# Edge blocks, Toeplitz copies, warm-up and instruction order in a convolution with routed experts

## The chip, the cores and the metric

The kernel runs on one core of a Trainium2 chip. The metric is the device time of one execution in microseconds (us), the median of several runs. The core has TensorE (PE; its weight loads are listed as PEld), VectorE (DVE), ScalarE (ACT), GpSimd (POOL) and SyncE (SP), each with a queue of its own that it works through in order, and 16 DMA engines. SP and POOL issue all transfers of this kernel: SP on the hardware queue, POOL on the software queue.

## The reference

```
x: 8 batches x 4160 positions x 192 channels, float32; weight: 8 heads x 7 taps
w = softmax(weight) over the taps                  # 24 channels belong to a head
y[b, s] = sum over k of w[h, k] * x[b, s - 6 + k]  # causal, zeros ahead of position 0
score[b, s] = y[b, s] . w_gate
for each batch: the 128 positions with the highest score
    h = max(y[top] @ w1, 0); ye = h @ w2           # 192 -> 1024 -> 192
    y[top] += sigmoid(score[top]) * ye
```

All of y is the output; only 128 rows of each batch are changed by the expert network.

## The kernel before

**Tiles.** A batch's 4160 positions are one edge block of 128 positions at its start and two groups of 18 windows of 112 positions. A group is written (b, g) here: (0,0), (0,1), (1,0), ... (7,1), 16 in all. A group lies in one of 10 buffers `xb`, a window's 118 positions (6 ahead of it) on the partitions, loaded by one DMA of 1728 KB (`load`). The buffers of the first six groups are used again by the last six. The 8 edge blocks lie together in `eb`.

**Convolution (`add_conv`, `add_edge`).** Per head a 128 x 128 matrix `toep` holds the seven weights along its diagonals. One product per head and group multiplies it with the head's 24 channels of 18 windows (432 columns); three PSUM banks (`pc`) take turns, and ScalarE copies each bank back into `xb`. The first group was cut into 10 and 18 - 10 windows (`CUT`), in two loads, and its first three heads in two products. The edge blocks take 8 products of 192 columns. In the trace a product is two records.

**Matrices.** VectorE and GpSimd make the taps' softmax and a `band` of shifted weights. Four products with selection matrices spread it over the partitions into two banks `pb` (two products each); from each bank, VectorE copies two of four 32-partition strips into `toep` and ScalarE the other two. `WARM` products on zeros run on TensorE ahead of this.

**Scores, search, expert network.** VectorE multiplies each window with `w_gate` and sums (`junk`, 18 per group, 8 for the edge blocks). When all scores of a batch are there, its search (`add_topk`) finds the 128th highest score by counting on ScalarE, TensorE and VectorE in turn, and the row indices `ix`. Then (`add_expert`) POOL gathers the rows from the output in DRAM (`xe`), TensorE transposes and multiplies by `w1s` and `w2s` (`px`, `ph`, `py`), and POOL scatters the result back. A gather reads the output, so it waits until the batch's two stores and the edge store have landed.

**Order.** Every operation is listed in `O` (class `Order`), and `SEQ` gives for each engine the order of the kinds: k constants, v convolution, x edge blocks, s scores, A to H the search of batch 0 to 7, a to h its expert network; on POOL ("G") l is a load; on SP z is a load of w1 or w2, p the edge store, w a group's store. `O.plan` merges the five strings by estimated times (`t0`, `since`, the costs in `add`) into one program; the strings alone fix each engine's order. The start, before the plan, issues `wt`, (0,0), `wg` and `eb` on SP and (0,1) on POOL.

Of the kernel before, what the change touches and what calls it, by code (L numbers as in the profile page):

```python
# [8 lines left out]
F32 = mybir.dt.float32  # L9
# [12 lines left out]

SEQ = {
    "PE": (
        "v10x8v19A2v3Av2AvAv2Av3A2v3Av3B2Av3Bv2BAv2AvBAv2Bv2B2v3BAv2Bv3Bv3BC2vBv2Cv4Cav2Ca3Cav3BC2a3Cav2Cv3D2"
        "a5Dv2CDa3v2Dv3CvbDv3D2Cv2DbCb2Dv3Dbv2DE2vDv2Ev5EvDcvc2Ec4Ecvcv2E2v2F2Eb2c2Fc3Eb3Eb7FEc3vEFv2FdvEvF2"
        "v3Fv4FGdGd3FGd2edGFd3FGd5GdeFe3G2eH2eGe2HGe2He2Ge2He2GfHGf2H2f2GHf2Hf2Hf4Hf2gHf2g3Hg11hg2h16"
    ),
    "A": (
        "v7x8v19A3v3Av2AvAv5A3v3Av3B3v3BAv2ABv2Bv5B3v2Bv3Bv3Bv3C3v4Cv2aC2v3a2v2C4vav3CvD4v3DCv3Dv3bv2D3vDv2D"  # L30
        "v3Dbv2bE3v5Ev2EcEvc2v3cvE3F3E2bFEv2Fv2Fvdv3F3v4Fv3FG3dGFGd2Ge2G3HeHGeHGHGHfH2fH2f2Hg4h4"
    ),
    "V": (
        "k13x3s7x3s29A2xA3s10A4s4A2s4As5A6s13ABABAxB3s8B4AsAs5BA3BAB2s4B2AB3As3A3s2BsBs4A2B2sAs5B2s2C3BC2BsB4"
        "C4sBs7C2s4aCBs2Cs5C5s11BC3B2as6DCD4s7D2sDs6CD2Cs2Das4D2s7bsCD2Cs2D3C6D2sCsCsCD2s2DsEsE3sD2Es5DsDbs2"
        "D2s2E2D2EDs9EsEs3DEs7E2cD2s4FEFcEsE2F2EFs15E3s4F2sEF2s4E2s5Es2bEFEFs3cEFE4F5EsEFs2EG3sFs4dFsGsGs3F2"
        "s7Gs2GsGFsGF2s5GF2Gs3FGdGF2sF2Gs2GFsGF2GdHGH3eH2G2HGH3GH2eH3G3H3G2HeHGH2GHG3H3G2H3GfH3fH10fH3g3h3"
    ),
    "G": (
        "l8al2blalcldlbecfdgehfgh"  # L40
    ),
    "SP": (
        "zpw2zw14"
    ),
}
LAT = {"PE": 197.0, "A": 162.0, "V": 135.0, "G": 150.0, "SP": 0.0, "Q": 0.0}
# [1 line left out]

RATE, BACK = 320.0, 340.0
FRESH = range(10)  # L50
WARM = 11


class Op:
# [123 lines left out]
def tile_conv_moe(ctx: ExitStack, tc: tile.TileContext, x, weight, w_gate, w1, w2, out, cap: int):  # L178
# [156 lines left out]
    HP = H // 4  # L335
# [31 lines left out]
    for j in range(HP):  # L367
        V.tensor_reduce(out=band0[:, j], in_=wp[:, j], axis=AX.X, op=ALU.add)
    V.tensor_tensor(out=band, in0=band0, in1=wr[:, :, None].to_broadcast([P, HP, NCc]), op=ALU.mult)
    HH = H // 2  # L370
    for half in range(2):
        pb = pf.tile([P, 512], F32, tag="pf", name=f"pb_{half}")
        for j in range(2):
            q = 2 * half + j
            PE.matmul(
                pb[:, j * HP * NCc : (j + 1) * HP * NCc], r32[:, q, :], band.rearrange("p j c -> p (j c)"),
                start=True, stop=True,
            )
# [167 lines left out]
    def add_conv(b, g):  # L546
        xt = xb[slot[b, g]]
        evs = []
        pss = [None] * H


        parts = [(h, 0, NI) for h in range(H)]
        if not evacs:
            parts = [(h, *c) for c in ((0, CUT), (CUT, NI)) for h in range(3)] + parts[3:]
        mms = {}
        for h, w0, w1 in parts:
            def mm(h=h, w0=w0, w1=w1):
                if w0 == 0:
                    pss[h] = pc.tile([P, 512], F32, tag="pc", name=f"pc_{b}_{g}_{h}")
                PE.matmul(  # L560
                    pss[h][:M, w0 * GC : w1 * GC].rearrange("p (w c) -> p w c", c=GC),
                    toep[: M + HALO, h, HALO : HALO + M], xt[: M + HALO, w0:w1, h * GC : (h + 1) * GC], start=True, stop=True,
                )

            m = O.add(
                "PE", pe((w1 - w0) * GC), mm, load_ops[b, g], kind="conv", takes="pc" if w0 == 0 else None, b=b,
                since=15000.0 if (b, g) == (0, 1) else 0.0,
            )
            mms.setdefault(h, []).append(m)
        for h in range(H):  # L570
            def ev(h=h):
                A.copy(xt[:M, :, h * GC : (h + 1) * GC], pss[h][:M, : NI * GC].rearrange("p (w c) -> p w c", c=GC))

            e = O.add("A", ca(NI * GC), ev, mms[h], kind="conv", drops="pc", b=b)
            evacs.append(e)
            evs.append(e)
        evac_ops[b, g] = evs
        score_ops[b, g] = [
            add_score(xt, 1 + NI * g + w, w, [evs[-1]], "score", b) for w in range(NI)
        ]  # L580

    def add_edge():

        evs = []
        for h in range(H):
            ps = {}
# [9 lines left out]
            m = O.add("PE", pe(B * GC), mm, [], kind="edge", takes="pc", since=17000.0)  # L596
# [278 lines left out]
    def add_expert(b, t, n, io):  # L875
# [4 lines left out]
        def add(eng, cost, fn, deps, **k):  # L880
            return O.add(eng, cost, fn, deps, kind=kind, b=b, **k)
# [42 lines left out]
        for f0 in range(0, NF, 4):  # L924
            mm = None
            for f in range(f0, f0 + 4):
                def h1(f=f, f0=f0):
                    if f == f0:
                        T["ph", f0] = pf.tile([P, 512], F32, tag="pf", name=f"ph_{b}_{t}_{f0}")
                    o = T["ph", f0].rearrange("p (f s) -> p f s", f=4)[:, f - f0, :n]  # L930
                    fs = slice(f * P, (f + 1) * P)
                    for c in range(DC):
                        PE.matmul(o, w1s[:, c, fs], T["xT"][:, c, :n], start=(c == 0), stop=(c == DC - 1))

                deps = [xo] + ([mm] if mm else [])
                mm = add("PE", 4 * 146.0 * n / P, h1, deps, takes="pf" if f == f0 else None)
# [83 lines left out]
```

## Time and profile before

| | |
|---|---|
| median of 3 runs | 206.16 us (206.03 to 206.88) |
| profiled execution | 204.77 us, its span 203.0 us |
| mean granted TensorE clock | 0.965 of full speed |
| busy: PE, DVE, ACT, POOL | 183.6, 159.4, 137.3, 44.0 us |
| moved by DMA | 58.15 MB, mean 286 GB/s |

The span goes from the first to the last instruction; the rest of the execution's time lies around it. Durations are in us, or in ns where marked. A line number is of little use here, because a helper issues every instruction (L189): the rows are told apart by their tiles, written out<-in. A row of the timeline gives start, length, engine, operation, tiles, form, the count of records merged in it, and in brackets the idle time ahead of it with what ended it. An engine name with a q is its queue of issues.

### The profile page before, as it was taken

The page shows a single profiled execution, that of the slowest core. Times are in us where ns is not written, and L with a number is a line of the kernel's source. Part 1 is how long each engine was busy: PE and PEld are TensorE (multiplying, and loading weights), DVE is VectorE, ACT ScalarE, POOL GpSimd, SP SyncE. Part 2 cuts the span into 40 slices and gives each one's busy share as a digit, 9 for nine tenths or more (in the row PEclk, how much of TensorE's full clock was granted, in tenths as well). Part 3 has the DMA queues.
Part 4 walks back from the last instruction along what each step waited for, and adds up shares of the span by engine and source line. Part 5 has one row for each costly group of instructions (what it writes and reads, how often), then busy time and mean ns, then how long its engine had stood idle before and what let it go on. Part 6 is the DMA issues. An engine that isn't in the chain of part 4 may idle for free. (4 is left out here: it accounts for less than half of the span.)

```text
span 203.0 us, 3660 instructions
## 1 busy us (share of the span) xinstructions
PE 183.6 (90%) x929; PEld 125.2 (62%) x929; DVE 159.4 (79%) x1099; ACT 137.3 (68%) x333; POOL 44.0 (22%) x85
## 2 busy tenths in 40 slices
PE   7396599998999998999999999999999989989990
PEld 2272574453554554575755655877656878879990
DVE  4690039999977997999998999999999997887200
ACT  2035157798999898787897897777789739462220
POOL 8987220000000033000304400320220110111311
PEclk9759679999999999999999999999999999999999
DMA  3999999999999999999999999999899999500100
GB/s 104 300 316 262 313 329 349 387 379 383 386 383 375 342 339 290 360 384 371 314 299 364 355 387 373 330 282 334 305 314 303 273 290 283 174 22 25 38 20 19
DMA packets 45284, 58.15 MB, mean 286 GB/s; under 512 B 1027, under 2 KB 39057, under 8 KB 45264
## 3 DMA queue, kind: packets, MB, share of 16 engines
q1 hardware_dynamic: 38464, 29.82, 47.3%
q0 software_dynamic: 6800, 28.11, 39.8%
q8 instruction: 7, 0.11, 0.2%
q14 instruction: 13, 0.11, 0.2%
HBM read 31.58 MB, written 26.35 MB: 285 GB/s over the span
## 5 line engine op out<-in xcount | busy, mean ns | idle before, releaser
L189 PE MATMUL pc<-xb,toep 118*112 118x432 f32 (+2 forms) x262 | 103.6, 537 | 0.7 <-ACT toep L189 0.5
L189 DVE SCALAR_TENSOR_TENSOR junk<-xb,wg 128x192 f32<-128x192 f32 x288 | 85.6, 352 | 0.3 <-ACT xb L189 0.3
L189 ACT COPY xb<-pc 112x432 f32<-112x432 f32 x128 | 61.7, 517 | 11.7 <-PE pc L189 10.9
L189 PEld LDWEIGHTS pc<-xb,toep 118*112 118x112 f32 x262 | 44.2, 183 | 33.0 <-issue 23.5
L189 ACT ACTIVATE sg<-rep,nb 128x592 bf16<-128x592 f32 (+1 forms) x48 | 36.3, 756 | 12.4 <-DVE j L189 11.7
L189 PE MATMUL ph<-xT,w1s 96*128 96x128 f32 x256 | 35.0, 282 | 0.0
L189 PEld LDWEIGHTS ph<-xT,w1s 96*128 96x128 f32 x256 | 31.1, 191 | 1.1 <-issue 0.5
L189 POOL DMA_INDIRECT xe<-out_dram,ix x8 | 8.2, 1022 | 101.8 <-DVE junk L189 62.6
L189 PE MATMUL py<-w2s,hT 128*128 128x192 f32 x128 | 24.8, 335 | 0.0
L189 DVE DVE_READ_ACCUMULATOR junk<-xb,wg 128x1 f32 x288 | 23.6, 82 | 0.0
L189 PE MATMUL tot<-gm,cnt 128*128 128x18 f32 x64 | 21.2, 337 | 2.6 <-ACT sg L189 2.2
L189 POOL DMA_DIRECT2D xb<-in_x_dram x16 | 19.4, 1219 | 8.6 <-PE pe L189 5.0
L189 PEld LDWEIGHTS tot<-gm,cnt 128*128 128x128 f32 x64 | 12.0, 188 | 14.0 <-ACT sg L189 11.7
L189 PEld LDWEIGHTS py<-w2s,hT 128*128 128x128 f32 x128 | 20.3, 190 | 0.0
L189 POOL DMA_INDIRECT out_dram<-res,ix x8 | 8.0, 997 | 43.9 <-DVE j L189 27.2
L189 DVE SCALAR_TENSOR_TENSOR j<-tot,inc 128x18 f32<-128x18 f32 x64 | 10.8, 174 | 6.6 <-PE tot L189 5.0
L189 ACT ACTIVATE hT<-ph 128x512 f32<-128x512 f32 x16 | 9.5, 593 | 9.4 <-PE ph L189 9.4
L189 ACT COPY rep<-pt 128x296 f32<-128x296 f32 x30 | 10.8, 412 | 5.1 <-PE pt L189 3.0
L189 PEld LDWEIGHTS <-e 128*128 128x128 bf16 x128 | 9.0, 97 | 6.6 <-issue 3.7
L189 PE MATMUL pt<-ex,e 128*128 128x148 bf16 x128 | 11.1, 227 | 1.5 <-DVE ex L189 1.4
L189 ACT ACTIVATE sg<-rep,b 128x592 bf16<-128x592 f32 (+1 forms) x16 | 12.1, 757 | 0.5
L189 DVE SCALAR_TENSOR_TENSOR junk<-eb,wg 128x192 f32<-128x192 f32 x8 | 2.5, 354 | 12.6 <-ACT eb L189 12.6
(110 smaller groups left out, 167.0 us busy)
## 6 DMA issues: line engine op xcount, KB each, us to landing
xb<-in_x_dram POOLq DMA_DIRECT2D x14, 1728.0 KB, 22.3
out_dram<-xb SPq DMA_DIRECT2D x16, 1512.0 KB, 22.1
xb<-in_x_dram POOLq DMA_DIRECT2D x1, 1632.0 KB, 14.3
xb<-in_x_dram SPq DMA_DIRECT2D x1, 960.0 KB, 6.6
xb<-in_x_dram SPq DMA_DIRECT2D x1, 768.0 KB, 8.4
eb<-in_x_dram SPq DMA_DIRECT2D x1, 768.0 KB, 16.8
w1s<-in_moe_w_dram SPq DMA_DIRECT2D x1, 768.0 KB, 21.3
out_dram<-eb SPq DMA_DIRECT2D x1, 768.0 KB, 20.7
```

Source lines behind the costliest of these rows:

```text
L189: return tc.keep_in_program_order(f(*a, **k))
```

## The change

The edge blocks are loaded and stored by one DMA per batch, 8 each way, where one DMA took all. The edge products, evictions and scores stand behind both groups of batch 0 in the order. The first group is one load and one product per head. The loads of w1 and w2 stand behind the stores of (0,0) and (0,1) on SP, and are listed with the edge store as what they come after. The matrices' four products go to four banks (three `pf`, one `pm`), and each bank is copied by one engine. There are 24 warm-up products. The load of (4,1) stands behind batch 0's gather on POOL ("l7al3" for "l8al2"). The strings for PE, A and V are new throughout, with the planner's estimates that they belong to.

```diff
     "PE": (
-        "v10x8v19A2v3Av2AvAv2Av3A2v3Av3B2Av3Bv2BAv2AvBAv2Bv2B2v3BAv2Bv3Bv3BC2vBv2Cv4Cav2Ca3Cav3BC2a3Cav2Cv3D2"
+        "v16x8v8A2v2Av2Av2Av2Av2A2v3Av3Av2Av2AB2v2BAv2Bv2BAv2Bv2B2v3Bv2Bv3Bv3CvCvBvCv2aCBa2Ca3BCv2C2a3vCv2Cva"
...
     "G": (
-        "l8al2blalcldlbecfdgehfgh"
+        "l7al3blalcldlbecfdgehfgh"
     ),
     "SP": (
-        "zpw2zw14"
+        "pwzwzw14"
     ),
...
-WARM = 11
+WARM = 24
...
-    CUT = 10
-    load(0, 0, 0, CUT)
-    load(0, 0, CUT, NI)
+    load(0, 0, 0, NI)
     SP.dma_start(wg, w_gate.partition_broadcast(P))
-    SP.dma_start(eb, bass.AP(x[0].tensor, x[0].offset, [[D, P], [S * D, B], [1, D]]))
+    for b in range(B):
+        SP.dma_start(eb[:, b, :], x[b][:P, :])
...
-    HH = H // 2
-    for half in range(2):
-        pb = pf.tile([P, 512], F32, tag="pf", name=f"pb_{half}")
-        for j in range(2):
-            q = 2 * half + j
-            PE.matmul(
-                pb[:, j * HP * NCc : (j + 1) * HP * NCc], r32[:, q, :], band.rearrange("p j c -> p (j c)"),
-                start=True, stop=True,
-            )
...
-            (A.copy if q > 1 else V.tensor_copy)(
...
+    for q in range(4):
+        pb = (pf if q < 3 else pm).tile([P, 512], F32, tag="pf" if q < 3 else "pm", name=f"pb_{q}")
+        PE.matmul(pb[:, : HP * NCc], r32[:, q, :], band.rearrange("p j c -> p (j c)"), start=True, stop=True)
+        pv = pb[:, : HP * NCc].rearrange("p (h c) -> p h c", c=NCc)
+        for k in range(4):
+            rows, lo, hi = slice(32 * k, 32 * k + 32), 32 * k, min(P, 32 * k + NCc)
+            (A.copy if q % 2 else V.tensor_copy)(toep[rows, HP * q : HP * q + HP, lo:hi], pv[rows, :, : hi - lo])
...
-        parts = [(h, 0, NI) for h in range(H)]
-        if not evacs:
-            parts = [(h, *c) for c in ((0, CUT), (CUT, NI)) for h in range(3)] + parts[3:]
...
-        dst = out[:, :P, :].rearrange("b p d -> p b d")
+        def st():
+            for b in range(B):
+                SP.dma_start(out[b][:P, :], eb[:, b, :])
...
     add_loads()
-    add_weights()
...
         if k == 1:
             add_edge()
+            add_weights()
```

## Rows read from the trace of the kernel before

**Rows 1.** The page: span, busy time by engine, two groups (count, busy, mean).
```profile
span 203.0 us, 3660 instructions
PE 183.6 (90%) x929; PEld 125.2 (62%) x929; DVE 159.4 (79%) x1099; ACT 137.3 (68%) x333; POOL 44.0 (22%) x85
...
L189 PE MATMUL ph<-xT,w1s 96*128 96x128 f32 x256 | 35.0, 282 | 0.0
...
L189 PE MATMUL py<-w2s,hT 128*128 128x192 f32 x128 | 24.8, 335 | 0.0
```

**Rows 2.** Stages: stretch, length, busy of PE, PEld, DVE, ACT, POOL (count); clock, DMA share, GB/s.
```profile
12.00:22.00 10.00, 6.37 (x19) 3.93 (x18) 3.56 (x30) 3.49 (x8) 6.40 (x25) 0.84 1.04 273
22.00:28.00 6.00, 5.47 (x17) 5.49 (x18) 0.00 (x0) 2.23 (x7) 1.23 (x1) 0.50 1.04 327
32.00:62.00 30.00, 28.99 (x105) 14.64 (x103) 28.32 (x201) 26.01 (x60) 0.00 (x0) 1.00 1.05 380
```

**Rows 3.** The chain of waits: the last piece of group (7,1)'s scores.
```profile
165.01 0.28 DVE junk L189 x2
```

**Rows 4.** Timeline of TensorE, 0 to 42 us.
```profile
1.24 4.14 PE L189 MATMUL pw<-xb 128*128 128x512 bf16 x11 [1.24 <-DVE xb L189]
8.77 1.96 PE L189 MATMUL pb<-band,xb 128*128 128x76 f32 x8 [3.39 <-DVE band L189]
11.23 7.14 PE L189 MATMUL pc<-xb,toep 118*112 118x240 f32 x20 [0.50 <-ACT toep L189]
22.53 5.46 PE L189 MATMUL pe<-eb,toep 128*128 128x192 f32 x16 [4.16 <-DMA eb<-in_x_dram]
27.78 14.24 PE L189 MATMUL pc<-xb,toep 118*112 118x432 f32 x38
```

**Rows 5.** Timeline of ScalarE: first matrix copies; first eviction of (1,0).
```profile
10.63 0.55 ACT L189 COPY toep<-pb 32x152 f32<-32x152 f32 x2 [4.37 <-DVE toep L189]
...
35.54 0.52 ACT L189 COPY xb<-pc 112x432 f32<-112x432 f32 x1 [0.21 <-PE pc L189]
```

**Rows 6.** Timeline of VectorE: its first score.
```profile
28.38 0.36 DVE L189 SCALAR_TENSOR_TENSOR junk<-eb,wg 128x192 f32<-128x192 f32 x1 [12.61 <-ACT eb L189]
```

**Rows 7.** DMA issues of 5 to 9 us (KB, us to landing); two in the timeline.
```profile
xb<-in_x_dram POOLq DMA_DIRECT2D x1, 1728.0 KB, 16.6
eb<-in_x_dram SPq DMA_DIRECT2D x1, 768.0 KB, 16.8
...
w1s<-in_moe_w_dram SPq DMA_DIRECT2D x1, 768.0 KB, 21.3
...
5.61 0.44 SPq L189 DMA_DIRECT2D eb<-in_x_dram  x1
...
5.59 1.46 POOL L189 DMA_DIRECT2D xb<-in_x_dram  x1
```

**Rows 8.** Timeline of POOL: batch 0's gather, the loads behind, the last load.
```profile
74.43 1.07 POOL L189 DMA_INDIRECT xe<-out_dram,ix  x1 [44.43 <-DVE junk L189]
75.48 2.51 POOL L189 DMA_DIRECT2D xb<-in_x_dram  x2
...
131.07 1.31 POOL L189 DMA_DIRECT2D xb<-in_x_dram  x1
```

**Rows 9.** Store (0,1): its issue on SP, and its us to landing.
```profile
35.36 23.35 SPq L189 DMA_DIRECT2D out_dram<-xb  x1
...
out_dram<-xb SPq DMA_DIRECT2D x1, 1512.0 KB, 38.0
```

**Rows 10.** Landing of the loads issued at 75.48 and 131.07 us.
```profile
xb<-in_x_dram POOLq DMA_DIRECT2D x1, 1728.0 KB, 15.4
...
xb<-in_x_dram POOLq DMA_DIRECT2D x1, 1632.0 KB, 14.3
```

**Rows 11.** Timeline of TensorE: into (4,1); first products of (7,1).
```profile
80.67 3.13 PE L189 MATMUL pc<-xb,toep 118*112 118x432 f32 x8
...
147.63 0.96 PE L189 MATMUL pc<-xb,toep 118*112 118x432 f32 x2
```

More of the change, by code (lines that the diff above doesn't have):

```diff
@@ L24 @@
     "PE": (
-        "v10x8v19A2v3Av2AvAv2Av3A2v3Av3B2Av3Bv2BAv2AvBAv2Bv2B2v3BAv2Bv3Bv3BC2vBv2Cv4Cav2Ca3Cav3BC2a3Cav2Cv3D2"
-        "a5Dv2CDa3v2Dv3CvbDv3D2Cv2DbCb2Dv3Dbv2DE2vDv2Ev5EvDcvc2Ec4Ecvcv2E2v2F2Eb2c2Fc3Eb3Eb7FEc3vEFv2FdvEvF2"
-        "v3Fv4FGdGd3FGd2edGFd3FGd5GdeFe3G2eH2eGe2HGe2He2Ge2He2GfHGf2H2f2GHf2Hf2Hf4Hf2gHf2g3Hg11hg2h16"
+        "v16x8v8A2v2Av2Av2Av2Av2A2v3Av3Av2Av2AB2v2BAv2Bv2BAv2Bv2B2v3Bv2Bv3Bv3CvCvBvCv2aCBa2Ca3BCv2C2a3vCv2Cva"
+        "CD2va4Dv2DCa3DCv2Dv5DCDv4Dbv2Dbv3Dv2DE2v2Eb3vDEv3DEv4Ev3cvc2vc4E2c2v2F2Eb4Eb4FvEb4FvEc3FdEc5vFv3EF2"
+        "v3Fv5FGdGFd3Gd2FdGdeFd4Ge4GFd4G2eH2Ge3HGe2HeGe2HGeHeGefH2f3HGf2Hf2Hf3Hf3Hfgf2g2Hg12hg2h16"
     ),
     "A": (
-        "v7x8v19A3v3Av2AvAv5A3v3Av3B3v3BAv2ABv2Bv5B3v2Bv3Bv3Bv3C3v4Cv2aC2v3a2v2C4vav3CvD4v3DCv3Dv3bv2D3vDv2D"
-        "v3Dbv2bE3v5Ev2EcEvc2v3cvE3F3E2bFEv2Fv2Fvdv3F3v4Fv3FG3dGFGd2Ge2G3HeHGeHGHGHfH2fH2f2Hg4h4"
+        "v16x8v8A3v2Av2AvAv5A3v4Av2Av2Av2B3v2Bv2BvBv5B3v3Bv2Bv4Bv2C3vCvaC2v2av3C3a2CvCv3D3CDvDv2Dv6Dv2D2v2bD"
+        "v4DvDv2E3vEv3Eb2v4Ev4cvcv3E2c2EF2EFbEvFEFvFvdv5F3v4Fv4FG3FGd3GeGeG3HeHGeHGHGHfH3fH2f2g4h4"
     ),
     "V": (
[L34 to L37, printed above, removed]
+        "k12s5ks26xs5x2A5xs5A4x3s2As4AsAs5A5s4As4xsAs2As8A3s5AB4sBs4A3B3sBs3A2BA3B3As2A2B5s9Bs2B2s4Bs6BC4BCs2"
+        "Bs9B2C3s9C2aBCB2C2B2sBC2BC3Bs10C2s5CDC2D3CDs4D3s3CD2aCsCaD3Cs7DCD4C3s2C2s7bD2s4DCs6Ds3D2E5D3s6E3s6ED"
+        "EDED3sD2E2Ds16Ebs5EF2E2FEF2s4cs2cs4E2s3Es3Es2F2s4FE2Fs6FEFEbEs5EF2E4FcF2sF2s2E2sEs4GFs4GFGFs8G2FdsF"
+        "s4Fs3FG3sGs2F2s3GFGF2dsGsF2s2GsGFGFGFGHdGH4eH2G3H3GHGH2eH2G2H3G2H4eHG3HGH2GHGH2G2H3fH5fH5fH3g3h3"
     ),
     "G": (
-        "l8al2blalcldlbecfdgehfgh"
+        "l7al3blalcldlbecfdgehfgh"
     ),
     "SP": (
-        "zpw2zw14"
+        "pwzwzw14"
     ),
@@ L549, in add_conv, with mm @@
         pss = [None] * H
-        parts = [(h, 0, NI) for h in range(H)]
-        if not evacs:
-            parts = [(h, *c) for c in ((0, CUT), (CUT, NI)) for h in range(3)] + parts[3:]
[L555 to L559, printed above, removed]
+        mms = []
+        for h in range(H):
+            def mm(h=h):
+                pss[h] = pc.tile([P, 512], F32, tag="pc", name=f"pc_{b}_{g}_{h}")
                 PE.matmul(
-                    pss[h][:M, w0 * GC : w1 * GC].rearrange("p (w c) -> p w c", c=GC),
-                    toep[: M + HALO, h, HALO : HALO + M], xt[: M + HALO, w0:w1, h * GC : (h + 1) * GC], start=True, stop=True,
-                )
-            m = O.add(
-                "PE", pe((w1 - w0) * GC), mm, load_ops[b, g], kind="conv", takes="pc" if w0 == 0 else None, b=b,
-                since=15000.0 if (b, g) == (0, 1) else 0.0,
+                    pss[h][:M, : NI * GC].rearrange("p (w c) -> p w c", c=GC), toep[: M + HALO, h, HALO : HALO + M],
+                    xt[: M + HALO, :, h * GC : (h + 1) * GC], start=True, stop=True,
+                )
+            mms.append(
+                O.add(
+                    "PE", pe(NI * GC), mm, load_ops[b, g], kind="conv", takes="pc", b=b,
+                    since=15500.0 if (b, g) == (0, 1) else 0.0,
+                )
             )
-            mms.setdefault(h, []).append(m)
         for h in range(H):
@@ L572, in ev @@
                 A.copy(xt[:M, :, h * GC : (h + 1) * GC], pss[h][:M, : NI * GC].rearrange("p (w c) -> p w c", c=GC))
-            e = O.add("A", ca(NI * GC), ev, mms[h], kind="conv", drops="pc", b=b)
+            e = O.add("A", ca(NI * GC), ev, [mms[h]], kind="conv", drops="pc", b=b)
             evacs.append(e)
@@ L594, in mm @@
                 )
-            m = O.add("PE", pe(B * GC), mm, [], kind="edge", takes="pc", since=17000.0)
+            m = O.add("PE", pe(B * GC), mm, [], kind="edge", takes="pc", since=20500.0)
             def ev(ps=ps, hs=hs):
@@ L603, in add_edge @@
             edge_scores.append(add_score(eb, 0, b, [evs[-1]], "edge", b))
-        dst = out[:, :P, :].rearrange("b p d -> p b d")
+        def st():
+            for b in range(B):
+                SP.dma_start(out[b][:P, :], eb[:, b, :])
         edge_stores.append(
-            O.add("SP", 0, lambda: SP.dma_start(dst, eb), [evs[-1]], kind="back", lat=1590.0, dma=B * P * D * 4 / BACK, cls=3)
+            O.add("SP", 0, st, [evs[-1]], kind="back", lat=1590.0, dma=B * P * D * 4 / BACK, cls=3, nd=B)
         )
@@ L935, in add_expert @@
                 deps = [xo] + ([mm] if mm else [])
-                mm = add("PE", 4 * 146.0 * n / P, h1, deps, takes="pf" if f == f0 else None)
+                mm = add("PE", 4 * 113.0 * n / P, h1, deps, takes="pf" if f == f0 else None)
             def rl(f0=f0):
@@ L991, in tile_conv_moe @@
             add_expert(b, t, n, hold[b][t])
-    t0 = {"PE": 11900.0, "A": 12300.0, "V": 11300.0, "SP": 4500.0, "G": 11500.0, "Q": 0.0, "D": 13500.0, "HW": 4500.0}
+    t0 = {"PE": 10300.0, "A": 11500.0, "V": 11600.0, "SP": 9000.0, "G": 8300.0, "Q": 0.0, "D": 15500.0, "HW": 9000.0}
     for op in O.plan(t0):
```

9 lines of the change are left out of this document (1 added, 8 removed).

## The prediction

> **What bounds the kernel now.** I read the page first, then the stages, the chain of waits, the timelines of the engines in the first 36 us, and the transfers one by one.
>
> The page says that TensorE is busy for 90% of the span and VectorE for 79% [rows 1]. The stage table says where: from 32 to 62 us TensorE has 28.99 of 30 us and VectorE 28.32, while the DMA engines stand at a share of 1.05 [rows 2]. So three resources are full at once, and a gain at the front reaches the end only if all three let it through. The chain of waits is VectorE's scores up to 165.3 (row at 165.01, 0.28 long) [rows 3]; behind them only the last batch's search and expert network follow. So I ask when the last group, (7,1), can start, because its scores are those.
>
> *The front.* TensorE makes 11 warm-up products (1.24 to 5.38), waits 3.39 for the band, makes the matrices' products, and runs (0,0) from 11.23 to 18.37. Then it is idle for 4.16 until the edge blocks have landed, runs their 8 products from 22.53 in 5.46 us, and is not idle again for long [rows 4]. VectorE idles 12.61 until 28.38 [rows 6]; ScalarE's first eviction of (1,0) is at 35.54 [rows 5]. The granted clock is 0.84 over 12 to 22 and 0.50 (that is 1.2 GHz) over 22 to 28 [rows 2]: it fell behind the idle stretch. Edge blocks and load (0,1) land together, 5.61 + 16.8 = 22.4 and 5.59 + 16.6 = 22.2; w1 is behind them in SP's queue and takes 21.3 [rows 7]. From 12 to 22, with these three at once, the DMA moves 273 GB/s; with one load at a time 327 (22 to 28); with loads and stores 380 [rows 2].
>
> *The back.* POOL's queue is in order, and gathers stand in it between loads. The gather of batch 0 at 74.43 is put down to VectorE, idle 44.43 [rows 8]; but store (0,1), issued at 35.36, lands 38.0 later, at 73.4 [rows 9], and that gather needs it. Two more, batches 1 and 3, start 0.8 us behind their second store in the same way. The last load is issued right behind batch 3's gather, at 131.07, and lands 14.3 later, 145.4 [rows 8, 10]; (7,1)'s first product is at 147.63 [rows 11]. So the last load hangs on bytes moved, not on TensorE, and only 2.2 us lie between it and its use.
>
> **The change part by part.**
>
> *Warm-up, 11 to 24 products.* 13 more at 4.14/11 = 0.38 each at most is 4.9 us: they end at 10.3 at the latest, against 8.77 when the band is ready [rows 4], so 1.5 us late; at the full clock from about where it rose before, they cost half and end in front of 8.77. The cover is the wait for load (0,1) below. I take 0 (0 to 1.5 lost).
>
> *Four banks.* Before, ScalarE's first copy waited 4.37, to the end behind VectorE's copies of the same bank [rows 5]. Its two copies of 0.55 us in all per bank (VectorE's are alike) become eight copies of half the columns on each engine, side by side. The first two heads' matrices are there up to 1 us sooner than 11.23; no copy makes TensorE wait, since a head's product takes 0.72. (0,0) as one load and in one piece per head saves three products' starts. All of it ends in front of load (0,1), so 0 as well (up to 1 us gained if that load came by 16).
>
> *Edge blocks and weights.* The edge load is 8 issues of 0.44 [rows 7] instead of one, so its last part leaves SP near 8.7 or later, with nothing queued behind it now; w1 and w2 go behind stores (0,0) and (0,1). Load (0,1) then shares the DMA with the edge blocks alone. From 12 to 22.2 some 2.78 MB moved at 273 GB/s; without w1's part (0 to 0.79 MB, I take 0.6, as it is three quarters through its 21.3 us) 2.18 MB remain: 8.0 us at 273, 6.7 at 327. So (0,1) lands at 18.7 to 20, at worst at 22.2. I take 18.8, the one-load rate, as 768-byte edge packets are few by then.
>
> *Order at the front.* (0,1) runs from 18.8: 8 products, 0.73 apart as in the stretch from 27.78 (19 in 14.24) [rows 4], to 24.6; then 8 edge products, 192 columns against 432, 0.36 each at full clock: 27.5; the first eviction of (1,0) follows one product later, at 28.3, where it was 35.54. That is 7.2 earlier at full clock, 5.0 if the edge products run at half (0.64 each, as before), 0.8 if load (0,1) is not sooner and the clock is as it was. Between (0,0)'s end (10.4 + 5.8 = 16.2) and 18.8 TensorE idles 2.6, less than the 3.39 and 4.16 behind which the clock fell. I take 6.0. VectorE can score (0,0) while TensorE runs (0,1), so its 12.61 shrink by as much.
>
> The Trainium skill, "TensorE: Matmul & The Clock Gate", section "HAM oscillation — how this bites in real kernels", warns that a wait for a transfer between two runs of products drops the array back to its cold clock and makes the next run start slow. The trace agrees for the wait of 4.16 [rows 2, 4]; by that rule (0,1) and the edges would again start at 1.2 GHz, the front would give some 2.6 instead of 6.0, and the sum below would lose 0.4.
>
> *The edge stores, the ninth load, the later order.* Eight edge stores hold SP 3.1 us longer; store (0,0) stands behind them. Before, a store's issue alone stood 23.35 us in SP because the queue was full [rows 9], so 0. Load (4,1) moves from before batch 0's gather to behind it; that gather's stores get one load less ahead of them (1.77 MB, 5.4 us at 327 GB/s), so I expect store (0,1) near 73.4 - 5.4 - 1.5 = 66.5. From there on POOL's and SP's order is as before, as is what TensorE has done by the end of (7,1).
>
> *The DMA's share.* Up to the last load the same bytes must move, so it comes sooner only by what was lost: 10 us at 273 instead of 327 GB/s are 0.54 MB, 1.5 us at the rates of [rows 2]. Bounds: 0 (two read queues stay at 273) to 2.8 (10 us at 380). To this comes the distance between landing and use, 147.63 - 145.4 = 2.2; the edge blocks were used 0.1 behind their landing [rows 4, 7], so up to 2.1 could go. I take 1.5, as the load's small last piece is issued behind its large one.
>
> *The sum.* The end moves by the smaller of front (6.0) and back (1.5 + 1.5): 3.0. The profiled execution took 204.77 us (span 203.0): 201.8. The median shown is 206.16, 1.4 above it; 3.0 less is **203.2**.
>
> **The rivals.**
>
> A. The front is carried whole: 6.0, time 200.2. For it: TensorE has hardly a hole after 27.78, and FFN 0 is issued earlier, so its scatter and the load behind it too. Against: the DMA share of 1.05 and the last load's 2 us. Chance 0.16.
>
> B. The transfers give nothing: the edge packets mix no better than w1's did, the last load lands where it did and is used as late, 206.0 (0 to 0.5 gained). For: w1's 0.79 MB only move elsewhere. Against: 273 GB/s stand alone among the stages. Chance 0.15.
>
> C. Slower: load (4,1) comes too late. If store (0,1) still lands at 73.4, the gather starts at 74.43 and three loads follow at 75.48 instead of two [rows 8]; the first of them lands 15.4 later [rows 10], at 90.9, and (4,1)'s products, at 82.9 before (the seventh of the eight records from 80.67) [rows 11], wait for it. A front 6.0 earlier would wait 14.0. The new order puts 8 more steps of expert network 0 (17 steps take (35.0 + 24.8)/8 = 7.5 [rows 1], so 3.5) and 9 of searches (some 2.2) ahead: 8.3 remain, 2.3 more than the front gave, 208.5. It decides from a store (0,1) landing at 71.1 on. Against: the 5.4 above. Chance 0.14.
>
> The Trainium skill, "DMA: Bandwidth & Descriptors", section "Bandwidth", asks for transfers of 1 MiB or more and gives each a fixed cost of about 2 us in "Anatomy of one DMA". Edge blocks in eight pieces of 96 KB go against it: 8 x 2.2 = 17.8 us one after another, an estimate from that page, instead of 3.8; stores behind would move towards C. No row here has such pieces back to back.
>
> **How the numbers follow.** Forecast 0.55, its own range 201.7 to 204.8 (from 1.4 gained, the distance alone, to 1.5 short of A); A 0.16, B 0.15, C 0.14. One measurement of this kernel tells about 0.5%, 1.0 us, from no change. Forecast and A are faster: 0.71; B is the same: 0.15; C slower: 0.14. The range takes in all of the forecast and B and the near parts of A and C: 200.3 to 206.9.
>
> **What would show it.** Right: load (0,1) landing near 19, TensorE idle there under 3 us with a granted clock of 1.0 behind it; first eviction of (1,0) near 28 to 30; batch 0's gather near 67; last load landing near 144 and used within 0.5 us; the scores' end near 162. Wrong: (1,0) not before 33 (the front failed); a hole on TensorE of several us before (4,1) (C); the last load at 145 or later (B) or before 141 (A).

## The result and the profile after

| | before | after |
|---|---|---|
| median of all runs side by side | 207.45 us (20 runs) | 204.90 us (20 runs) |
| ratio of after to before | | 0.985 (0.981 to 0.989) |
| profiled execution, its span | 204.77, 203.0 us | 201.73, 199.9 us |
| mean granted TensorE clock | 0.965 | 0.985 |

The kernel is 1.5% faster. The forecast was 203.2 of 206.16 us, a ratio of 0.986. The spans differ by 3.1 us, where the sum had 3.0. The same total does not mean the same terms, though, and the two traces differ from the sum in every large one.

Executions of one kernel fall into a faster and a slower group, so each ratio compares the faster ones alone, and the profile of after is that of a second run of the changed kernel (e0 below), because the first fell in the slower group. Medians here are of all runs and spread by a few us; below I compare marks within single traces more than medians.

The stages of after (columns as in [rows 2]):

```profile
12.00:22.00 10.00, 7.94 (x20) 3.57 (x19) 8.83 (x65) 4.88 (x10) 7.30 (x36) 0.89 1.06 327
22.00:28.00 6.00, 4.57 (x12) 2.08 (x11) 1.60 (x13) 2.89 (x6) 0.00 (x0) 0.89 1.05 327
32.00:62.00 30.00, 29.53 (x109) 14.11 (x107) 26.16 (x188) 26.90 (x64) 0.00 (x0) 1.00 1.05 362
```

The DMA moves 327 GB/s from 12 to 22 where it moved 273, VectorE has 8.83 us of work there instead of 3.56, and the clock over 22 to 28 is 0.89 instead of 0.50 [rows 2]. TensorE of after, first the front and then into (7,1):

```profile
1.23 7.80 PE L189 MATMUL pw<-xb 128*128 128x512 bf16 x24 [1.23 <-DVE xb L189]
8.87 1.01 PE L189 MATMUL pb<-band,xb 128*128 128x76 f32 x8
10.39 6.03 PE L189 MATMUL pc<-xb,toep 118*112 118x432 f32 x16 [0.51 <-DMA xb<-in_x_dram]
18.48 7.72 PE L189 MATMUL pc<-xb,toep 118*112 118x432 f32 x16 [2.06 <-DMA xb<-in_x_dram]
27.63 2.89 PE L189 MATMUL pe<-eb,toep 128*128 128x192 f32 x16 [1.43 <-ACT xb L189]
30.36 5.97 PE L189 MATMUL pc<-xb,toep 118*112 118x432 f32 x16
...
144.98 0.69 PE L189 MATMUL pt<-ex,e 128*128 128x148 bf16 x8
145.52 2.37 PE L189 MATMUL pc<-xb,toep 118*112 118x432 f32 x6
```

(0,1) starts at 18.48, idle 2.06 ahead of it. But between the end of (0,1) and the edge products there is a second hole, which the sum did not have. It is put down to ScalarE; ScalarE had been done by then, and the edge blocks' pieces were late. SP's timeline and the list of issues:

```profile
5.77 6.06 SPq L189 DMA_DIRECT2D eb<-in_x_dram  x8
...
eb<-in_x_dram SPq DMA_DIRECT2D x8, 96.0 KB, 9.3
```

The 8 issues take 6.06 us, the last of them near 11.5. Of the first six pieces, four have a landing in the records, 9.3 us behind the issue by the median, and the later the longer (5.9 to 14.7). The last piece's landing is missing in this trace; in the five kernels below whose records hold it (e5, e7, e9, e10, e11) it is at 26.8 to 27.8, and the edge products start 0.3 us behind it each time. ScalarE of after, with the matrix copies (now at once with VectorE's; it waited 4.37 for them in [rows 5]), the edge evictions and the first eviction of (1,0):

```profile
9.47 1.78 ACT L189 COPY toep<-pb 32x76 f32<-32x76 f32 x8 [3.64 <-PE pb L189]
...
28.23 2.65 ACT L189 COPY eb<-pe 128x192 f32<-128x192 f32 x8 [1.48 <-PE pe L189]
31.29 0.52 ACT L189 COPY xb<-pc 112x432 f32<-112x432 f32 x1 [0.41 <-PE pc L189]
```

VectorE of after, its first score (28.38 in [rows 6]) and the end of the last score of (7,1) ([rows 3]):

```profile
17.00 0.36 DVE L189 SCALAR_TENSOR_TENSOR junk<-xb,wg 128x192 f32<-128x192 f32 x1 [0.90 <-ACT xb L189]
...
161.25 0.08 DVE L189 DVE_READ_ACCUMULATOR junk<-xb,wg 128x1 f32 x1
```

POOL of after: the gather of batch 0 with three loads behind it, the last loads, and the tail (gathers `xe`, scatters `res`):

```profile
69.61 1.07 POOL L189 DMA_INDIRECT xe<-out_dram,ix  x1 [49.39 <-DVE junk L189]
70.66 3.72 POOL L189 DMA_DIRECT2D xb<-in_x_dram  x3
...
129.78 1.90 POOL L189 DMA_DIRECT2D xb<-in_x_dram  x2
...
171.49 0.99 POOL L189 DMA_INDIRECT out_dram<-res,ix  x1 [8.01 <-DVE j L189]
178.41 0.97 POOL L189 DMA_INDIRECT xe<-out_dram,ix  x1 [5.93 <-DVE fjunk L189]
181.33 0.99 POOL L189 DMA_INDIRECT out_dram<-res,ix  x1 [1.94 <-DMA xe<-out_dram,ix]
184.55 0.97 POOL L189 DMA_INDIRECT xe<-out_dram,ix  x1 [2.23 <-DVE fjunk L189]
```

From these rows the path can be laid down mark by mark:

| mark | before | after | gained up to here |
|---|---|---|---|
| first eviction of (1,0) | 35.54 | 31.29 | 4.25 |
| first product of (7,1) | 147.63 | 145.52 | 2.11 |
| end of (7,1)'s scores | 165.29 | 161.33 | 3.96 |
| end of the span | 203.0 | 199.9 | 3.1 |

So 4.25 us are gained at the front, not 6.0. Between (1,0) and (7,1) the new order takes 2 us longer, and from (7,1) to the last score 1.85 us less (15.81 for 17.66, of which VectorE is busy 15.53 and 16.96); the last batch's search and expert network then lose 0.9 again. The questions for the experiments: did the front or the last load decide when (7,1) starts, what made the front's size, which edits were worth nothing, and where the 0.9 went.

### The profile page after: what moved, and what is told of

Same layout as the page of the kernel before. It is cut to its first block, busy times and chain, and to the rows that moved or that the text cites. A ratio compares the mean times of both kernels' runs of the same rounds, so it can differ in the third digit from the quotient of the medians.

```text
span 204.0 us, 3714 instructions
## 1 busy us (share of the span) xinstructions
PE 188.1 (92%) x936; PEld 123.9 (61%) x936; DVE 161.2 (79%) x1103; ACT 137.6 (67%) x337; POOL 44.3 (22%) x85
## 3 DMA queue, kind: packets, MB, share of 16 engines
HBM read 31.58 MB, written 26.35 MB: 284 GB/s over the span
## 4 chain that ended last, share of the span: by engine, by line
PE 36%; DVE 8%; DMA 4%; ACT 3%; issue 3%; POOLq 1%; ACTq 0%; DVEq 0%
PE pc L189 18%; PE ph L189 8%; PE py L189 5%; DVE junk L189 3%; PE tot L189 3%; ACT sg L189 3%; DMA out_dram<-res,ix 2%; PE pt L189 2%; DMA xe<-out_dram,ix 1%; DVE j L189 1%; DVE inc L189 1%; POOLq L1005 1%; DVE sv L189 1%; PE pi L189 1%; PE px L189 0%
## 5 line engine op out<-in xcount | busy, mean ns | idle before, releaser
L189 PE MATMUL pc<-xb,toep 118*112 118x432 f32 x256 | 103.2, 538 | 3.9 <-DMA xb<-in_x_dram 2.0
L189 PEld LDWEIGHTS pc<-xb,toep 118*112 118x112 f32 x256 | 41.6, 178 | 35.7 <-issue 25.3
L189 PE MATMUL ph<-xT,w1s 96*128 96x128 f32 x256 | 33.8, 281 | 0.4 <-ACT xT L189 0.4
L189 POOL DMA_INDIRECT xe<-out_dram,ix x8 | 8.4, 1051 | 114.0 <-DVE inc L189 57.2
L189 PEld LDWEIGHTS ph<-xT,w1s 96*128 96x128 f32 x256 | 30.5, 191 | 1.5 <-ACT xT L189 0.9
L189 PE MATMUL py<-w2s,hT 128*128 128x192 f32 x128 | 26.4, 344 | 0.0
L189 PEld LDWEIGHTS py<-w2s,hT 128*128 128x128 f32 x128 | 20.9, 194 | 1.0 <-issue 0.9
L189 PE MATMUL tot<-gm,cnt 128*128 128x18 f32 x64 | 19.9, 315 | 1.5 <-ACT sg L189 1.0
L189 DVE SCALAR_TENSOR_TENSOR j<-tot,inc 128x18 f32<-128x18 f32 x64 | 11.2, 174 | 7.3 <-PE tot L189 5.6
L189 PE MATMUL pt<-ex,e 128*128 128x148 bf16 x128 | 11.9, 231 | 0.3
L189 DVE TENSOR_SCALAR inc<-nb,dj 128x1 f32<-128x1 f32 x48 | 9.8, 209 | 0.6
## 6 DMA issues: line engine op xcount, KB each, us to landing
out_dram<-xb SPq DMA_DIRECT2D x16, 1512.0 KB, 21.4
eb<-in_x_dram SPq DMA_DIRECT2D x8, 96.0 KB, 11.3
```

Source lines behind the costliest of these rows:

```text
L189: return tc.keep_in_program_order(f(*a, **k))
```

## The experiments

Theory F: the front decides, and whatever it gives arrives at (7,1) until the last load lands too late. Theory B (the prediction's rival and its bound): the bytes decide, by the last load's landing. The expectations call this R (rival); from the kernels with fewer bytes on they call B that both limits hold, the later one. The new strings, the four banks and the eight edge stores were not undone by themselves in any run. Diffs are against the changed kernel unless told otherwise.

**The changed kernel again** (e0), for its spread.

> The changed kernel as it is, for a second profile: the first showed the edge products from 28.3 us, 3.6 us of idle TensorE ahead of them, and the clock at 1.2 GHz from 27.3 to 34.1. Theory F (the front decides: the end moves by as much as the first product of (1,0) moves): where the clock stays up there, the edge products take about 2.7 us instead of 5.5, (1,0) starts near 31 instead of 33.5, and the time is about 203. Rival R (the back decides: the last load's landing caps the gain, as the prediction said): the same time with and without the clock's fall, and the last load used within 0.5 us of its landing. Ratio to before 0.981 to 0.989 by both.

Measured: 205.33 us against 208.42, ratio 0.984 (0.974 to 0.994); its profile stands above.

**Edge blocks in one load** (e1).

```diff
-    for b in range(B):
-        SP.dma_start(eb[:, b, :], x[b][:P, :])
+    SP.dma_start(eb, bass.AP(x[0].tensor, x[0].offset, [[D, P], [S * D, B], [1, D]]))
```

> Undoes one part: the edge blocks come in one DMA, as before, the rest stays. F: all its descriptors are queued by 8 us, most edge packets move ahead of load (0,1), the edge blocks are there by 20 us, no wait behind (0,1), (1,0) starts at 27 to 28 us, and the time falls by 3 to 5 us against the changed kernel, to 198 to 200. R: the front gains the same 5 us, but the last load lands within 1 us of where it did and the time falls by less than 1 us. A third: one DMA is no sooner than eight, edge blocks still land near 27, no difference.

Measured: ratio 0.984 (0.979 to 0.990), no different from eight pieces. Its list of issues and its TensorE:

```profile
eb<-in_x_dram SPq DMA_DIRECT2D x1, 768.0 KB, 15.6
```

```profile
19.21 8.99 PE L189 MATMUL pc<-xb,toep 118*112 118x432 f32 x16 [2.84 <-DMA xb<-in_x_dram]
28.03 3.02 PE L189 MATMUL pe<-eb,toep 128*128 128x192 f32 x16
```

Issued at 5.8, the one load lands at 21.4, some 6 us ahead of the last of eight pieces, and the edge products follow (0,1) without a hole. But (0,1) takes 8.99 us instead of 6.0, because most of it ran at half clock, and what the earlier landing gave is gone: (1,0) came at 31.82, so the early front that F and R differ over was not there.

**Eleven warm-up products** (e2).

```diff
-WARM = 24
+WARM = 11
```

> Undoes one part: 11 warm-up products instead of 24. F: (0,0) runs partly at 1.2 GHz and ends near 18, when load (0,1) lands at 18.5, so at most 0.5 us of the front is lost and the edge wait covers it: within 0.7 us of the changed kernel, unless the clock is then low in (0,1) as well, which would cost up to 3 us. R: no difference.

Measured: ratio 0.986 (0.974 to 0.999); part of (0,0) at half clock, and yet the first eviction of (1,0) at 31.69, within 0.4 of after. The 13 products are worth nothing here: with eleven, the last eviction of (0,0) is at 19.45, behind the landing of load (0,1) at 18.2, but the wait for the edge blocks, 2.82 us ahead of their products at 28.04, covers that.

**Load (4,1) back ahead of batch 0's gather** (e3).

```diff
-        "l7al3blalcldlbecfdgehfgh"
+        "l8al2blalcldlbecfdgehfgh"
```

> Undoes one part: load (4,1) again stands ahead of batch 0's gather on POOL (l8al2). F: TensorE's order is unchanged, batch 0's gather comes some 5 us later (near 74 instead of 69.6) as one more load is ahead of its stores, and FFN 0, which the new order has before (4,1), starts up to 3 us later: time up by 0 to 2 us. R: the same bytes ahead of the last load: within 0.5 us.

Measured: 207.46 us (6 runs, too few for a ratio). POOL of this kernel:

```profile
74.25 1.23 POOL L189 DMA_INDIRECT xe<-out_dram,ix  x1 [48.26 <-DVE inc L189]
75.47 2.51 POOL L189 DMA_DIRECT2D xb<-in_x_dram  x2
```

The gather is at 74.25 again, as before the change [rows 8]; with the load behind it, it is at 69.61. The load's 1.77 MB held up store (0,1), as the prediction's 5.4 us said in kind: it landed at 73.3 here and at 68.6 in the first profile of after, whose (1,0) came later still (34.7, and 33.3 here). What it does to the time is not settled.

**The front without holes: one edge load, and products on zeros in the two waits** (e4).

```diff
+    def filler(n):
+        if n:
+            t = pm.tile([P, 512], F32, tag="pm", name="fill")
+            for k in range(n):
+                PE.matmul(t, warm[:, :P], warm, start=True, stop=True)
...
+                if (b, g, h) == (0, 1, 0):
+                    filler(9)
...
+                if h == 0:
+                    filler(2)
```

> The changed kernel with the edge blocks in one DMA, and 9 products on zeros ahead of (0,1)'s first product and 2 ahead of the edges' so that TensorE's clock has no reason to fall in the wait for load (0,1). With the clock up, (0,1) runs from 19 to 25, the edge blocks have landed at 21.4 (as in the run with one load), (1,0)'s first eviction is near 28.5 instead of 31.3. F (the end follows the front): (7,1)'s first product comes 114 us behind that eviction as in the five profiles so far (113.9 to 114.4), near 142.7, and the end is 2.5 to 3 us sooner than in the repeated changed kernel (span 199.9): 197. R (the last load caps it): (7,1) not before 145, no gain.

Measured: 203.76 against 207.83 us, ratio 0.990 (0.983 to 0.997), no different from after. Its front has the 6 us that the prediction asked for, and TensorE now waits for loads, the last time ahead of (7,1) (TensorE, then the last load's line in the list of issues, issued at 129.75):

```profile
16.42 2.11 PE L189 MATMUL fill<-xb 128*128 128x512 bf16 x8
18.96 6.03 PE L189 MATMUL pc<-xb,toep 118*112 118x432 f32 x16 [0.43 <-DMA xb<-in_x_dram]
...
25.26 2.82 PE L189 MATMUL pe<-eb,toep 128*128 128x192 f32 x16
27.91 5.96 PE L189 MATMUL pc<-xb,toep 118*112 118x432 f32 x16
...
84.16 0.95 PE L189 MATMUL pc<-xb,toep 118*112 118x432 f32 x2 [0.86 <-ACT hT L189]
...
109.43 0.95 PE L189 MATMUL pc<-xb,toep 118*112 118x432 f32 x2 [0.28 <-DMA xb<-in_x_dram]
...
145.16 2.40 PE L189 MATMUL pc<-xb,toep 118*112 118x432 f32 x6 [0.50 <-DMA xb<-in_x_dram]
```

```profile
xb<-in_x_dram POOLq DMA_DIRECT2D x1, 1632.0 KB, 14.9
```

The clock was 1.00 over the front and on to (7,1), and the first eviction of (1,0) was at 28.84, 6.7 us earlier than before. After's distance from there to (7,1), 114.2, would have given 143.1; the last loads landed at 144.7 and 145.0, and (7,1) started at 145.16. Of 2.45 us more at the front 0.36 arrived. The last load did not take all of the rest, though: by the first evictions of each group, the lead over after shrinks by 0.9 at (4,1) (the row at 84.16; its load, issued at 69.15 behind batch 0's gather, landed at 84.02, and ScalarE's `hT` ended then too), by some 0.5 at (6,0) (109.43, load landed at 109.3), and the rest goes at the last load, for which TensorE waits 0.50. So the bytes bind at three places here; in after, (4,1) had some 0.5 us to spare.

**The same with fewer bytes (e8), and after with fewer bytes (e9).** In both, the load of (5,0) brings only 9 of its 18 windows, 0.86 MB less, so that part of the output is not the reference's.

```diff
-            ... lambda: load(b, g, 0, NI, G), ...
+            ... lambda: load(b, g, 0, 9 if (b, g) == (5, 0) else NI, G), ...
```

> The kernel with one edge load and filler products, and 0.86 MB less to move: load (5,0) brings 9 of its 18 windows, the others keep an older group's values (so that part of the output is not the reference's). Two limits at once (new theory B: (7,1) starts at the later of the first eviction of (1,0) + 114.2 and the last load's landing + 0.1): the landing moves from 145.0 to about 142.7, the front gives 28.8 + 114.2 = 143.0, so (7,1) starts near 143.1 instead of 145.2, the scores end 15.9 later, near 159, and the time falls by 2 us or a little more. F alone (TensorE only): (7,1) was then already as early as it can be, no change. R alone (bytes only): the same 2.3 us as B.

> The same 0.86 MB less in the changed kernel itself, without the filler and with the edge blocks in eight pieces. B and F: the first eviction of (1,0) stays at 31.3 or later, so (7,1) stays at 145.5 or later (114 behind it); the time falls by at most the end's share, where the last stores drain 2.4 us sooner (0 to 1 us). R alone: (7,1) near 143, time 2.3 us down.

Measured: 202.93 us (no ratio) and 203.07 us (ratio 0.979, 0.973 to 0.984) against 207.93. TensorE and the last load's line (issued at 127.07) with the early front and fewer bytes, and then TensorE with after's front and fewer bytes:

```profile
143.20 0.69 PE L189 MATMUL pt<-ex,e 128*128 128x148 bf16 x8
143.74 2.37 PE L189 MATMUL pc<-xb,toep 118*112 118x432 f32 x6
```

```profile
xb<-in_x_dram POOLq DMA_DIRECT2D x1, 1632.0 KB, 13.6
```

```profile
144.63 0.69 PE L189 MATMUL pt<-ex,e 128*128 128x148 bf16 x8
145.16 2.37 PE L189 MATMUL pc<-xb,toep 118*112 118x432 f32 x6
```

With the early front, the landing of loads was what held (7,1): here the last one lands at 140.7 (144.7 above), the wait for (6,0) is gone too, and (7,1) starts at 143.74, 1.42 us earlier, behind TensorE's own products and with no wait. With after's front the same bytes change next to nothing (145.16 for 145.52, and (1,0) was 0.24 earlier). The two fronts differ by 1.36 us ((1,0) at 29.69 and 31.05) and the two starts of (7,1) by 1.42. So both theories hold, each on its side: (7,1) starts at the later of (1,0) + 114.1 and what the loads allow, of which the last one's landing is the latest. The first of the two limits has more behind it than these two traces: in seven of the traces of the changed order (both of after, e1, e2, e3, e8 and e9) the distance is 114.0 to 114.4 us, with (1,0) anywhere from 29.69 to 34.74; in the others TensorE waits for transfers on the way (e4, and e5, e7, e10 and e11 below). After stands just on the front's side, with the two limits about 0.4 us apart, if its last load, issued at 129.78, landed as the one issued at 129.75 above did (its own landing is not in the records).

The medians of these two kernels do not tell them apart; the rows do. And 0.86 MB less did not move the landing by the 2.3 us expected: against e4's 144.7 it came 4.0 us sooner with the early front, but only 0.4 sooner (144.3) with after's, where the load was issued at 130.36, behind batch 3's gather. So the landing hangs on when that gather lets the load go, and not on the bytes alone.

**More bytes** (e5). The store of (1,0) is issued a second time, into the place of (7,0), 1.55 MB.

```diff
+        def put():
+            SP.dma_start(dst, src[:M])
+            if (b, g) == (1, 0):
+                SP.dma_start(far, src[:M])
```

> The changed kernel with one more store: group (1,0) is stored a second time, to a place of the output that a later store overwrites (1.55 MB, 4.1 to 4.7 us of the DMA engines at 330 to 380 GB/s), behind its own store on SP. F: nothing on TensorE's path is later by more than slack, time within 1 us. R: every load and store behind it is 4 to 5 us later; the last load and (7,1) with them: time 3 to 5 us up. If it is 1 to 3, both limits are close together.

Measured: ratio 1.022 (1.009 to 1.035). POOL and TensorE:

```profile
99.20 1.27 POOL L189 DMA_INDIRECT xe<-out_dram,ix  x1 [24.80 <-DVE d L189]
```

```profile
110.01 0.66 PE L189 MATMUL px<-ident,xe 128*96 128x128 f32 x2 [5.55 <-DMA xe<-out_dram,ix]
```

The gather of batch 1 came at 99.20 (94.56 in after), and TensorE, whose queue is in order, stood 5.55 us at that batch's transposes; the clock fell behind it. (7,1) started at 152.2, 6.7 us late. Bytes ahead of a gather cost more than their own 4.3 us (at the 362 GB/s of after's third stage), so more than either theory had, and by another way: the wait for a gather.

**The kernel before with the weights late** (e6), the one edit alone (against before).

```diff
-        "zpw2zw14"
+        "pwzwzw14"
```

> The kernel before with one part of the change alone: w1 and w2 behind the edge store and stores (0,0), (0,1). Load (0,1) lands near 18.5 to 19 instead of 22.2. The edge blocks, still ahead in TensorE's order and in one DMA, land at 17 to 21. F: the edge products start 2 to 4 us sooner than 22.5, (1,0)'s first eviction moves by as much, and so does the end: ratio 0.98 to 0.99. R: the DMA gain of 1.5 us plus the distance to the last load's use, ratio 0.985 to 0.995.

Measured: 207.04 (4 runs, too few for a ratio) against 207.83 us. TensorE, and the last load's line (issued at 131.93):

```profile
21.40 2.89 PE L189 MATMUL pe<-eb,toep 128*128 128x192 f32 x16 [1.83 <-DMA eb<-in_x_dram]
...
81.23 0.42 PE L189 MATMUL px<-ident,xe 128*96 128x128 f32 x2 [2.14 <-DMA xe<-out_dram,ix]
...
146.69 0.96 PE L189 MATMUL pc<-xb,toep 118*112 118x432 f32 x2
```

```profile
xb<-in_x_dram POOLq DMA_DIRECT2D x1, 1632.0 KB, 13.5
```

This edit alone gives 4.0 us at the front (the first eviction of (1,0) at 31.58) and 0.9 at (7,1). The last load lands where it landed before, at 145.5, but TensorE does not wait for it; what it waits for, in this execution, is batch 0's gather, 2.14 us at 81.23, and the clock is down behind that (0.57 from 83 to 86). From (7,1)'s first product to the last score it takes 17.66 us, exactly as before. So the late weights alone give nearly as much at the front as the whole change (4.25), and the new order's 1.85 us come from the strings. What the edit is worth in time is not settled.

**The changed kernel with the weights early** (e7).

```diff
-        "pwzwzw14"
+        "zpw2zw14"
```

> The changed kernel with that part undone: w1 again right behind the edge loads, the edge store and the rest of SP's order as before the change. Load (0,1) lands at 21 to 22 instead of 18.4, the edge blocks later than 28. F: (1,0)'s first eviction at 34 to 36 and time up by 3 to 4 us against the repeated changed kernel, about the kernel before. R: 1.5 us up.

Measured: ratio 0.997 (0.988 to 1.007). So no gain over the kernel before is shown any more, though the range just reaches that of after (0.981 to 0.989). TensorE in the profiled execution, 209.88 us, the longest of eleven:

```profile
82.58 0.63 PE L189 MATMUL px<-ident,xe 128*96 128x128 f32 x2 [2.60 <-DMA xe<-out_dram,ix]
```

The price did not come where I had looked for it. (0,1) still landed at 17.4; w1 is issued only at 11.2, behind the eight edge issues. Batch 0's gather, issued at 71.29, took 11.1 us (6.2 in after), TensorE waited 2.60 for it, and the clock was at its lower level for 10 us from there. But this is not shown to come from the early weights: the last kernel below, whose program is that of the changed kernel up to this point, has the same in its trace, a gather of 11.3 us and TensorE's wait for it:

```profile
79.85 0.59 PE L189 MATMUL px<-ident,xe 128*96 128x128 f32 x2 [2.00 <-DMA xe<-out_dram,ix]
```

So what the early weights cost, and where, stays open.

**Eight pieces and products on zeros in both waits** (e10; 8 and 13 products).

> The changed kernel with the edge blocks in eight pieces, and filler products alone: 8 ahead of (0,1)'s first product, 13 ahead of the edges'. The clock stays at 2.4 GHz over the front in every run; the edge products still wait for the last pieces, near 27.7, and (1,0)'s first eviction stays at 31.0 to 31.3. B: (7,1) near 145.4, time as in the undisturbed runs of the changed kernel (202 to 203), never with the front of 34.7 that its first profile had.

Measured: ratio 0.985 (0.973 to 0.998), the time of after. The clock stayed at 1.00 over the front, but (1,0) came at 31.72: the edge products waited for the last piece all the same (28.06). Two later waits for transfers, in TensorE's rows,

```profile
106.17 0.42 PE L189 MATMUL px<-ident,xe 128*96 128x128 f32 x2 [0.88 <-DMA xe<-out_dram,ix]
...
121.23 2.40 PE L189 MATMUL pc<-xb,toep 118*112 118x432 f32 x6 [0.29 <-DMA xb<-in_x_dram]
```

make up most of the way from 31.72 + 114.1 = 145.8 to 147.35, where (7,1) started in this one execution; 145.4 had been expected.

**More at the end** (e11). Half of the store of (7,0) goes out twice.

```diff
+        def put():
+            SP.dma_start(dst, src[:M])
+            if (b, g) == (7, 0):
+                SP.dma_start(dst[:, :9], src[:M, :9])
```

> The changed kernel, with half of the store of (7,0) (9 of 18 windows, 0.77 MB) issued a second time right behind it, so that only the last stores grow. Theory: the 0.9 us that the changed kernel loses behind the scores' end (38.6 us from the scores' end to the span's end, against 37.7 before) are lost because batch 6's gather stands in POOL's queue behind batch 3's scatter, whose rows share the DMA with the last stores. Then the scatter lands some 2 us later, batch 6's gather starts 2 us later than its 1.4 us behind the row indices, and the distance from the scores' end to the span's end grows from 38.6 to about 40.6. Rival: the loss lies in the new order of searches on VectorE; then that distance stays at 38.6 whatever the stores do.

Measured: 208.35 us (4 runs, too few for a ratio). In the profiled execution, 209.44 us, the last score ends at 167.12 and the span at 207.35, a distance of 40.2. POOL's tail:

```profile
177.17 0.99 POOL L189 DMA_INDIRECT out_dram<-res,ix  x1 [7.86 <-DVE j L189]
183.84 1.08 POOL L189 DMA_INDIRECT xe<-out_dram,ix  x1 [5.68 <-DVE sv L189]
```

The distance is 1.6 more than in after, near the theory's 2.0, but that decides nothing: without any more bytes at the end it is 38.7 in e9, 39.4 in e4 and 40.8 in e1. Nor did the theory's path come: the scatter of batch 3 and the gather behind it are 6.67 apart (6.92 in after). And row indices of batch 6 are ready 15.6 us behind the last score in both, against 14.9 before (180.20), which no store explains. The distance is 37.7 in both traces of the old order (the kernel before, and the one with the weights late) and at least 38.6 in every trace of the new one, so that part of the 0.9 goes with the new order. Of after's 0.9, 0.5 stands ahead of the last gather (184.55, for 188.04 before) and 0.4 behind it; what makes it stays open.

## Why the prediction was right, and where its terms were not

*Warm-up 0, four banks 0:* right. Copies run side by side, (0,0) starts at 10.39, and load (0,1) covers all of it; eleven products give the same front, there by the cover of the edge blocks' wait. The four banks were not undone by themselves.

*Load (0,1) at 18.8, idle 2.6:* right (landed at 18.3, used at 18.48, idle 2.06), and so is the reason, 327 GB/s with the weights gone: that edit alone took the landing from 22.2 to 18.5 in the kernel before. In the changed kernel the eight edge issues keep w1 away as well (17.4 with the weights early).

*The edge blocks:* this step failed. The prediction had them in SBUF when (0,1) ended at 24.6, "as 768-byte edge packets are few by then". They were half of all packets. In 13 to 18 us of after, the queues moved:

```profile
q0 software_dynamic: 323, 1.41, 88.6%
q1 hardware_dynamic: 321, 0.22, 17.7%
```

Columns are packets, MB and share. The two queues get packet for packet the same number, so the edge pieces of 768 bytes a packet get about a seventh of the bytes beside a load (0.22 of 1.63 MB). The Trainium skill, "DMA: Bandwidth & Descriptors", section "Queues, rings and completion order", says that an engine takes turns between queues by the packet; the trace agrees, 321 to 323 (which records make up one packet in the Trainium skill's sense it does not show). The last piece so landed at 26.8 to 27.8, and the edge products of after were at 27.63 instead of 24.6. One load, whose packets are all queued from the start, landed at 21.4 (e1): from 10 to 12 us, with load (0,1) only starting, its queue moved 0.52 MB, where the eight pieces' queue moved 0.10. The prediction's other reading, eight pieces one after another at some 2 us each, is not what the trace shows: in e9 the first two pieces land 0.3 us apart (11.8 and 12.1), and only the last six, beside the load, 2.1 to 2.4 apart.

*The clock:* the prediction took full speed, since 2.6 us of idle were less than what the clock had fallen behind. This step failed as well; the traces show both cases. In after it was low from 19.9 to 23.3, behind 2.06 us of idle, and the edges ran at full speed; in the first profile of the same kernel it stayed up in (0,1) and fell for the edges, so that (1,0) came at 34.7 and only 0.8 of the front was left. That this is the lowest of the prediction's three values is chance, since that value was for a load (0,1) that is not sooner. TensorE and a stage (clock 0.56) of that first profile:

```profile
18.64 6.03 PE L189 MATMUL pc<-xb,toep 118*112 118x432 f32 x16 [2.04 <-DMA xb<-in_x_dram]
28.28 5.46 PE L189 MATMUL pe<-eb,toep 128*128 128x192 f32 x16 [3.61 <-issue]
```

```profile
28.00:35.00 7.00, 6.72 (x20) 6.03 (x21) 1.84 (x15) 2.81 (x9) 0.00 (x0) 0.56 1.04 327
```

The Trainium skill, "TensorE: Matmul & The Clock Gate", section "HAM oscillation — how this bites in real kernels", the rule that was weighed, would have had both (0,1) and the edges start cold: the edges did in the first profile, (0,1) started at full clock in both and fell 1.4 us into its run in after, and with products on zeros in the waits neither started cold. Length of the wait alone did not decide: of two kernels with the front of after, the edges ran at full clock behind 3.73 us of idle in one (e5, (1,0) at 30.90) and partly at half clock behind 3.78 in the other (e3, 33.30). The front's size is then 7.2 at full clock, less 3.0 for the late edge blocks: 4.2, where I had taken 6.0. The clock cost after nothing, since (0,1) ran its slow part while the edge blocks were still on their way; in the first profile, where it fell later, (1,0) came 3.5 later.

*Eight edge stores 0, load (4,1) behind the gather:* no run undoes the edge stores by themselves, so their 0 is not tested; nor does the row show why a store's issue stood 23.35 us in SP before. The load's move was right in direction: the gather of batch 0 was at 69.6 (forecast 67; 74.43 before), so store (0,1) had landed before the 71.1 from which rival C decides, and C's hole did not come; with the earlier front of e4, (4,1) did wait for that load, by 0.9.

*The back, 3.0:* its two terms were mis-sized against each other. The load's large piece landed at 145.41 before, the small one behind it, which (7,1) needs too, at 145.75, so the distance to the use was 1.9 and not 2.2. Where the load decided (e4), the pieces landed 0.7 sooner, at 144.7 and 145.03, and the distance fell to 0.1 (145.16): 0.7 where 1.5 was taken for the bytes' share, and 1.75 where 1.5 was taken for the distance. Together 2.5, for 3.0.

*The sum, the smaller of front and back:* the rule is right, as the two kernels with fewer bytes show, but at (7,1) the smaller of the two was the front, with 2.1, and not the back, with 2.5. Two terms stood at nothing that were not nothing. First the new order: by "as is what TensorE has done by the end of (7,1)" it was to change nothing, but the way from (1,0) to (7,1) became 2.1 us longer. TensorE is idle there as little as before (2.3 us for 2.5) and has eight more records of the search (`pt`) in it, worth some 0.5; what makes the rest is not shown. In return VectorE has 1.4 us less to do beside the scores from (7,1) on, and these ended 3.96 earlier. The second is the 0.9 lost in the tail. 2.1 + 1.85 - 0.9 = 3.1 is what happened; 3.0 was reached by a smaller back, no new order and no tail. The total was closer than its parts deserved, and that is luck.

*The signs:* load (0,1) near 19, idle under 3 and the scores' end near 162 (161.3) came as said. (1,0) at 28 to 30 was missed by 1.3, the gather near 67 by 2.6, and the clock of 1.0 behind the idle stretch did not hold (0.50 from 20 to 23). "The last load at 145 or later" was named as the sign of B; where the records hold its landing with all bytes moved (e4, e10), it stood near that edge or behind it (144.7, 146.1) without B coming true, since the distance to its use had gone.

## What to carry to other kernels

Where an early start and a late transfer both bound the last stage, lay the two down as times of one mark, and see by how much the second stands behind the first: gains above that are not paid out (here 0.36 of 2.45 us), and look at the loads in between as well as at the last. A transfer in small packets beside one in large ones got its share by packets here, not by bytes, so queue it whole and early, or put nothing large beside it. A gather that lands late stops TensorE in its queue and can take the clock down with it, so look for such waits in each trace before a difference is put down to an edit: the same wait stood in kernels with and without the early weights. When an order is written anew, compare distances between marks along the whole run; work that moves past the mark one looks at changes its time without any gain.

## What the hardware showed that I had not expected

- Two queues with packets of 768 and about 4400 bytes moved 321 and 323 packets in the same 5 us (48 of them under 512 bytes), so 0.22 and 1.41 MB.
- The last of eight pieces of 96 KB, issued over 6.06 us, landed at 26.8 to 27.8; the same bytes in one issue at 20.7 to 21.6 (e1, e4, e8), with 326 to 330 GB/s in all from 12 to 22 us in both ways.
- The clock fell behind idle stretches of 2.06 and 3.61 us in some executions and stayed up behind 2.04 and 3.73 us in others with the same front, with up to 3.5 us between the first evictions of (1,0) of one kernel (31.29 and 34.74).
- 1.55 MB more, ahead of a gather, cost 6.7 us at the last group: the wait stood in TensorE's queue, and the clock fell behind it.
